# A third group of seven products in row block 3's first matmul, in place of four dense blocks

## The chip, the cores and the metric

The kernel runs on one core of a Trainium2 chip. The metric is device time in microseconds. Before the change it is 268.82 us, the median of three runs (268.22 to 269.44).

## What is computed

Two parts follow one another. Attention runs inside chunks of 64 tokens, for 8 batches, 8 heads, 576 tokens and head size 64. Its output is laid out as 4608 rows of 512 and goes through a two-layer network with an exact gelu:

```
q_c, k_c, v_c = (a.reshape(B, H, nc, 64, D) for a in (q, k, v))
scores = scale * np.matmul(q_c, k_c.transpose(0, 1, 2, 4, 3))
attn = softmax(scores)
out = np.matmul(attn, v_c)

x = out.transpose(0, 2, 1, 3).reshape(4608, 512)
h = x @ w_in                       # 512 -> 2048
g = 0.5 * h * (1 + erf(h / sqrt(2)))
return g @ w_out                   # 2048 -> 512
```

## The kernel before

**Row blocks.** The 4608 rows are worked in nine row blocks of 512, indices 0 to 8 (`t` in the code). Blocks 0 to 7 are the first 512 tokens of each batch, block 8 is the last chunk of all batches. For each block there are three stages: attention, which gives `x` transposed; mm1, which gives the gelu of h in a tile `h` of 16 feature blocks of 128 by 512 tokens; and mm2, which gives the output rows. Attention of block t+1 (and the scores of t+2) is laid in pieces between the steps of mm2 of block t.

**mm1 of one dense feature block** (`mm1_slot`, line 455): four matmuls of 512 columns, one for each quarter of the 512 inputs, into one PSUM bank. A gelu on ScalarE (ACT) takes the bank to `h` (line 457).

**mm1 by seven products** (`seven_rows`, line 573): four feature blocks at a time form a group. The group is a matrix of two by two blocks, and its product with the two-by-two blocks of x is made from seven block products in place of eight, the way of Strassen and Winograd. Each product is four matmuls of 256 columns on TensorE (PE). The sums that it needs are made ahead on VectorE (DVE): sums of w_in once for each group (`w_in_sums`), sums of x once for each row block (`x_sums`, line 556). The rest are steps of the group, named in the order lists:

- p1, p2, p3, p4, p6, p7: a product, added into a PSUM bank called a, b or d. p3 ends with the gelu of block (1, 0).
- p5: a product into d, and a copy on ACT of d into a tile in SBUF, `kept_p5` (line 585).
- s11: a copy on ACT of bank a to bank b (line 586). c11, c12, c22: gelus on ACT (line 581).
- s12: d becomes a + kept, on DVE (line 577). c22+: kept becomes a + kept, on DVE.

One prime on a name stands for the second group (feature blocks 4 to 7), two for the third (8 to 11), three for the fourth (12 to 15). A number in a list is a dense feature block.

**What sets the order.** Everything stands in a manual schedule: each engine works its instructions strictly in the order in which the program names them, and `mm1_seven` runs down one list for each row block. Other names in the lists are hooks: x is the x sums, k the copies of k by chunk for block 4 together with block 5's k transpose and the next loads, g0 sums of g for mm2 and two rounds of w_in sums.

**Banks and homes.** PSUM has eight banks in three pools: `mm` and `at` with three, `tp` with two. A new tile takes the place that was freed first, and waits until it is free. The kept tiles of groups one and two are in the pool `work`. From row block 5 on there are two more homes, `kept_more`, in a tile that is put aside in row block 4 (`kept_home`). The pool `ypool` has four tiles of 128 x 512 f32; mm2 uses four of them for each row block, for three kept products and the last one. Each of them is freed by the store of its quarter to HBM (`store_block`, line 743), which goes through the queue of SyncE (SP), in the order of the program, like nearly all loads.

**mm2** (`mm2_seven`, line 731) is one such group of seven over the whole block: first a product kept by a copy on ACT (line 691), then one into bank b, then five with sums. The third needs the first bank free, that is, the copy done. Row blocks 2 to 8 have mm1 with two or more groups. In row block 3 (`T0`), before the change, groups one and two are products and blocks 8 to 15 are dense.

Of the kernel before, what the change touches and what calls it, by code (L numbers as in the profile page):

```python
# [11 lines left out]
def kernel(  # L12
# [10 lines left out]
    P = 128  # L23
    f32 = mybir.dt.float32
# [14 lines left out]
    NT = B + 1  # L39
# [52 lines left out]
    ypool = ctx.enter_context(tc.tile_pool(name="ypool", bufs=4))  # L92
# [123 lines left out]
    AT, TP, MM = (ps_at, "at"), (ps_tp, "tp"), (ps_mm, "mm")  # L216
# [233 lines left out]
    def mm1_slot(t, f):  # L450
# [3 lines left out]
        for ks in range(KS):  # L454
# [5 lines left out]
    T0 = 3  # L460
    DENSE = (0,)
    TWICE = tuple(range(2, NT))
    THRICE = tuple(range(T0 + 2, NT))
    FOURTH = ("p1", "s11", 11, "p1'", "p2", "s11'", "c11", "p6", 9, "p5'", "p5", "p6'", 14, "s12'", "s12", "p2'", 13, 10, "p4'",
# [4 lines left out]
    LATER = ("p1", "s11", "p5", "p1'", "p1''", "p2", "p6", "c11", "s11'", "s11''", 13, "s12", 14, "p2''", "c11''", "p6'", "p4",  # L469
# [18 lines left out]
    LAST = ("p1", "p5", "s11", 13, 14, "p1'", "s11'", "p2", "c11", "p6", "p1''", "s11''", 15, "p5'", "s12", "p7", "p2''", "c22+",  # L488
# [3 lines left out]
    FOUR = {NT - 3: SIXTH, NT - 2: SEVENTH}  # L492
    WHOLE = {**FOUR, T0 + 1: FOURTH, NT - 1: LAST, T0 + 2: LATER}

    HF = FF // 2
    HD = d_model // 2
    HM = MT // P // 2
# [20 lines left out]
    def w_in_block(r, c, of=0):  # L518
        n = HD * (2 * of + r)
        return w_in_sb[:, 2 * c:2 * c + 2, n:n + HD]  # L520

    def x_block(t, r, c):
        return tiles[t]["x"][:, 2 * r:2 * r + 2, HD * c:HD * (c + 1)]

    def x_sum(i):
        return flat(k_bds[3 - (i - 1) // 2], 4)[:, (i - 1) % 2 * 2:(i - 1) % 2 * 2 + 2]
# [4 lines left out]
    kept_more = []  # L531
# [26 lines left out]
    def seven_rows(t, of, pools, kept, bank):  # L558

        h = tiles[t]["h"]  # L560
        w, ws = lambda r, c: w_in_block(r, c, of), w_in_sum[of]

        def place_of(to):
            if to not in bank:
                pool, tag = pools[to]
                bank[to] = pool.tile([P, HM, HD], f32, tag=tag, name="hs_ps")
            return bank[to]

        def product(to, left, right, fresh=False):
            hs = place_of(to)  # L570
            for f in range(HM):
                for ks in range(2):
                    nc.tensor.matmul(hs[:, f], left[:, ks, f * P:(f + 1) * P], right[:, ks],  # L573
                                     start=(fresh and f == 0 and ks == 0), stop=(ks == 1), skip_group_check=True)

        def plus(to, src):
            nc.vector.tensor_tensor(to, bank[src][:], kept, op=ADD)  # L577

        def gelu(r, c, src):
            n = HM * (2 * of + r)  # L580
            nc.scalar.activation(h[:, n:n + HM, HD * c:HD * (c + 1)], src, Act.Gelu)  # L581

        return {
            "p1": lambda: product("a", w(0, 0), x_block(t, 0, 0), True),
            "p5": lambda: (product("d", ws[0], x_sum(1), True), AC(kept, bank["d"][:])),
            "s11": lambda: AC(place_of("b")[:], bank["a"][:]),
            "p2": lambda: product("b", w(0, 1), x_block(t, 1, 0)),
            "c11": lambda: gelu(0, 0, bank["b"][:]),
            "p6": lambda: product("a", ws[1], x_sum(2)),
            "s12": lambda: plus(bank["d"][:], "a"),  # L590
            "p4": lambda: product("d", ws[3], x_block(t, 1, 1)),
            "c12": lambda: gelu(0, 1, bank["d"][:]),
            "p7": lambda: product("a", ws[2], x_sum(3)),
            "c22+": lambda: plus(kept, "a"),
            "c22": lambda: gelu(1, 1, kept),
            "p3": lambda: (product("a", w(1, 1), x_sum(4)), gelu(1, 0, bank["a"][:]))}

    def mm1_seven(t, hooks):

        if t > 1:  # L600
            tiles[t]["h"] = hpool.tile([P, FF, MT], bf16, tag="h", name="h")
        kept = [work.tile([P, HM, HD], f32, tag="t1", name="kept_p5", bufs=2)[:] for _ in range(2 if t in TWICE else 1)]
        bank, more, third, fourth = {}, {}, {}, {}
        if t == 1:
            does = seven_rows(t, 1, {"a": TP, "b": AT, "d": AT}, kept[0], bank)
        else:
            does = seven_rows(t, 0, {"a": AT, "b": AT, "d": AT}, kept[0], bank)
        if t in TWICE:
            does.update((step + "'", do) for step, do in
                        seven_rows(t, 1, {"a": TP, "b": TP, "d": AT}, kept[1], more).items())  # L610
            if t not in WHOLE:
                fifth = does["p5'"]
                does["p5'"] = lambda: (more.update(d=bank["b"]), fifth())
        if t in THRICE:
            pools = dict.fromkeys("abd", MM) if t == NT - 1 else {"a": MM, "b": AT, "d": AT}
            does.update((step + "''", do) for step, do in seven_rows(t, 2, pools, kept_more[0], third).items())
        if t in FOUR:
            does.update((step + "''", do) for step, do in seven_rows(t, 2, dict.fromkeys("abd", MM), kept_more[0], third).items())
            does.update((step + "'''", do) for step, do in
                        seven_rows(t, 3, {"a": MM, "b": AT, "d": MM} if t == NT - 2 else {"a": MM, "b": MM, "d": AT},  # L620
                                   kept_more[1], fourth).items())
        if t in WHOLE:
            order = WHOLE[t][:WHOLE[t].index("Y0")]
        elif t == T0:
            order = ("p1'", "s11'", "x", "p1", "s11", 8, 10, "k", "p6'", "p2", "c11", 11, "p6", "p5", "p5'", "p2'", "c11'", 9, 13,
                     "s12", "p7", "s12'", "p4", "c22+", "p7'", "c12", "c22", "p4'", "c12'", 15, "p3", "c22+'", "p3'", "c22'", 12,
                     "g0", 14)
        elif t == 2:
            order = ("p1", "s11", "p1'", "x", "u0", "s11'", 8, "p2", "c11", "p5", 9, "p6", "s12", "p5'", "p6'", "s12'", 10, "p7", 11,
                     "c22+", "c22", "p7'", 12, "p4", "c12", "p3", "c22+'", "p3'", 13, "p4'", "p2'", "u1", "k", "c22'", "c11'", "c12'",  # L630
                     "g0", 14, 15, "s3")
        else:
            order = (9, "p1", "s11", 10, 11, "w", "p5", "p2", "c11", "p6", 12, "s12", "w0", "p4", "p7", "c12", "c22+", "w1", 13,
                     "c22", "p3", 14, "g0", "s3", 15)
        for step in order:
            if step in does:
                does[step]()
                continue
            for u in hooks.get(step, ()):
                u()  # L640
            if not isinstance(step, str):
                mm1_slot(t, step)
# [224 lines left out]
    with tc.manual_schedule():  # L867
# [46 lines left out]
        p2 = att_sum_pe(0, 2)  # L914
        p3 = att_sum_pe(0, 3)
# [63 lines left out]
        def whole_hooks(t):  # L979
# [16 lines left out]
            e1, e2, slot = {}, {}, 0  # L996
            for step in WHOLE[t]:
                if str(step)[0] == "Y":
# [26 lines left out]
        for t in range(1, NT):  # L1025
# [46 lines left out]
            if t <= T0:  # L1072
# [24 lines left out]
                else:  # L1097
# [3 lines left out]
                    e2[13] = parts[1]  # L1101
            if t in WHOLE:
                e1, e2 = whole_hooks(t)
# [29 lines left out]
```

## Time and profile before

| | us |
|---|---|
| median of 3 runs | 268.82 |
| the profiled execution | 269.02 |
| its span, first to last instruction | 267.2 |
| PE busy | 258.7 (97%) |
| DVE busy | 220.8 (83%) |
| ACT busy | 199.1 (75%) |
| POOL busy | 87.8 (33%) |
| mm1 of row block 3 on PE | 106.18 to 119.29 |

The granted clock of PE is 1.00 throughout. Busy time is that in which an engine's datapath works; a wait is not counted in it. In a timeline, a group's length runs from its first start to its last end, and neighbours overlap, so the distance between two starts is what one more instruction costs. In the chain of work that ended last, each piece was released by the one ahead of it. SPq is the queue in which SP issues transfers; its landing is the time at which the transfer's semaphore tells that it is done.

### The profile page before, as it was taken

Reading aid. Unit: us, or ns where it says so; the run is one execution under the profiler, and the core shown is the slowest. Engines: PE = TensorE matmul, PEld = TensorE weight load, DVE = VectorE, ACT = ScalarE, POOL = GpSimd, SP = SyncE. Lnnn points to the kernel's source line nnn. Section 1 sums busy time; section 2 is a strip of 40 time slices with the busy share of each in tenths; the row PEclk is TensorE's granted clock in tenths of the full one; section 3 lists DMA queues with packets and bytes.
Section 4 is the critical chain, followed back from the end, with each engine's and each line's share of the span. In section 5 each row is a group of like instructions: output and inputs, shape, how many; then the busy total and the mean of one; then the engine's idle time right before and its main releaser. Section 6 shows DMA issues by size and latency. Waiting matters only on the chain.

```text
span 267.2 us, 7499 instructions
## 1 busy us (share of the span) xinstructions
PE 258.7 (97%) x3025; PEld 201.2 (75%) x3025; DVE 220.8 (83%) x373; ACT 199.1 (75%) x388; POOL 87.8 (33%) x142
## 2 busy tenths in 40 slices
PE   6699999999999999999999999999999999999994
PEld 2478775556886688668876887788888888887883
DVE  6874687989996899988998899898999999943752
ACT  3767758888676967789977987897799789228810
POOL 7878668701177210921712910304200300000000
PEclk9999999999999999999999999999999999999999
DMA  6999998999699899999899729999954320120014
GB/s 188 293 336 403 391 403 201 292 179 277 195 383 254 183 226 296 245 250 333 221 257 328 184 84 175 204 151 174 254 125 93 96 81 2 42 91 28 4 39 118
DMA packets 104739, 53.97 MB, mean 202 GB/s; under 512 B 72960, under 2 KB 101632, under 8 KB 104704
## 3 DMA queue, kind: packets, MB, share of 16 engines
q1 hardware_dynamic: 104400, 53.23, 76.6%
q8 instruction: 23, 0.38, 0.6%
q10 hardware_dynamic: 304, 0.26, 0.3%
q14 instruction: 12, 0.10, 0.1%
HBM read 36.70 MB, written 9.44 MB: 173 GB/s over the span
## 4 chain that ended last, share of the span: by engine, by line
PE 66%; DMA 14%; SPq 7%; DVE 6%; ACT 3%; issue 1%; POOL 1%; DVEq 0%; POOLq 0%
PE y_ps L731 27%; PE hs_ps L573 22%; PE h_ps L455 9%; DMA arrival<-in_moe_w_out_dram 5%; DMA arrival<-in_k_dram 5%; DMA arrival<-in_moe_w_in_dram 3%; SPq L157 2%; SPq L118 2%; SPq L128 2%; PE h_ps L445 2%; DMA k_t<-k_nat 1%; PE y_ps L801 1%; PE y_ps L765 1%; DVE k_bd L667 1%; PE av_ps L312 1%
## 5 line engine op out<-in xcount | busy, mean ns | idle before, releaser
L731 PEld LDWEIGHTS <-h 128*128 128x128 bf16 x384 | 37.1, 98 | 5.1 <-issue 0.4
L457 ACT ACTIVATE h<-h_ps 128x512 bf16<-128x512 f32 x53 | 31.7, 601 | 11.8 <-PE h_ps L455 7.7
L581 ACT ACTIVATE h<-hs_ps 128x512 bf16<-128x512 f32 x63 | 36.0, 602 | 3.7 <-PE hs_ps L573 3.4
L455 PE MATMUL h_ps<-x,w_in_sb 128*128 128x512 bf16 x156 | 38.6, 379 | 0.0
L164 POOL CAST q_nat<-arrival 128x512 bf16<-128x512 f32 x31 | 20.0, 686 | 52.3 <-DMA arrival<-in_q_dram 38.6
L214 POOL CAST v_nat<-arrival 128x1024 bf16<-128x1024 f32 x14 | 15.9, 1146 | 45.3 <-DMA arrival<-in_v_dram 45.3
L731 PE MATMUL y_ps<-v_bd,k_bd 128*128 128x256 bf16 x256 | 29.8, 273 | 0.2
L731 PE MATMUL y_ps<-w_out_sb,h 128*128 128x256 bf16 x256 | 29.8, 273 | 0.0
L573 PEld LDWEIGHTS <-w_in_sb 128*128 128x128 bf16 x252 | 24.6, 98 | 4.6 <-issue 0.2
L731 PEld LDWEIGHTS <-k_bd 128*128 128x128 bf16 x256 | 24.8, 98 | 3.7 <-issue 0.2
L164 POOL CAST k_nat<-arrival 128x512 bf16<-128x512 f32 x30 | 20.2, 706 | 17.3 <-DMA arrival<-in_v_dram 13.2
L455 PEld LDWEIGHTS <-w_in_sb 128*128 128x128 bf16 x156 | 15.3, 98 | 12.2
L573 PE MATMUL hs_ps<-x,w_in_sb 128*128 128x256 bf16 x168 | 23.6, 273 | 0.0
L696 DVE TENSOR_TENSOR kept<-y_ps,kept 128x512 f32<-128x512 f32 (+1 forms) x25 | 16.4, 656 | 6.7 <-issue 4.2
L865 ACT ACT_TABLE_LOAD x16 | 20.5, 1283 | 1.0 <-PEq L1117 0.7
L691 ACT COPY kept<-y_ps 128x512 f32<-128x512 f32 (+1 forms) x26 | 14.4, 558 | 9.2 <-PE y_ps L731 8.9
L577 DVE TENSOR_TENSOR hs_ps<-hs_ps,kept_p 128x512 f32<-128x512 f32 x15 | 10.2, 693 | 7.6 <-PE hs_ps L573 6.7
L731 PE MATMUL y_ps<-v_bd,s_sb 128*128 128x256 bf16 x128 | 15.8, 273 | 0.0
L246 ACT ACTIVATE pT<-s_ps 128x512 bf16<-128x512 f32 x28 | 14.4, 599 | 1.6 <-PE s_ps L239 1.6
L731 PE MATMUL y_ps<-v_bd,h 128*128 128x256 bf16 x128 | 15.3, 272 | 0.1
L573 PEld LDWEIGHTS <-w_in_more 128*128 128x128 bf16 x128 | 12.5, 98 | 3.7 <-issue 0.3
L731 PE MATMUL y_ps<-w_out_sb,s 128*128 128x256 bf16 x128 | 15.3, 273 | 0.0
(144 smaller groups left out, 553.0 us busy)
## 6 DMA issues: line engine op xcount, KB each, us to landing
arrival<-in_v_dram SPq DMA_DIRECT2D x58, 128.0 KB, 4.2
arrival<-in_q_dram SPq DMA_DIRECT2D x7, 1024.0 KB, 6.1
arrival<-in_k_dram SPq DMA_DIRECT2D x6, 1024.0 KB, 8.1
out_dram<-kept SPq DMA_DIRECT2D x21, 256.0 KB, 2.5
arrival<-in_moe_w_out_dram SPq DMA_DIRECT2D x4, 1024.0 KB, 12.1
arrival<-in_moe_w_in_dram SPq DMA_DIRECT2D x6, 512.0 KB, 6.5
out_dram<-y_sb SPq DMA_DIRECT2D x11, 256.0 KB, 3.0
arrival<-in_k_dram SPq DMA_DIRECT2D x8, 256.0 KB, 5.6
```

The lines of the kernel that those rows point to most:

```text
L164: copy(st[nm][:, g].rearrange("p j r d -> p r j d"), st[nm + "f"][:, 2 * g:2 * g + 2])
L214: copy(st["v"][:, r::2], st["vf"][:, r::2])
L246: nc.scalar.activation(pT[:].rearrange("p u (c j) -> p u c j", j=J), s_ps[g2][c][:].rearrange("p u (j c) -> p u c j", j=J), Act.Exp, scale ...
L455: (nc.tensor.matmul if t else by_halves)(h_ps[:], w_in_sb[:, ks, f * P:(f + 1) * P], tiles[t]["x"][:, ks, :], start=(ks == 0), stop=(ks == ...
L457: nc.scalar.activation(tiles[t]["h"][:, f, :], h_ps[:], Act.Gelu)
L573: nc.tensor.matmul(hs[:, f], left[:, ks, f * P:(f + 1) * P], right[:, ks], start=(fresh and f == 0 and ks == 0), stop=(ks == 1), skip_grou ...
L577: nc.vector.tensor_tensor(to, bank[src][:], kept, op=ADD)
L581: nc.scalar.activation(h[:, n:n + HM, HD * c:HD * (c + 1)], src, Act.Gelu)
L691: nc.scalar.copy(kept[name][:, ms], ps[:])
L696: nc.vector.tensor_tensor(y_sb[:, ms], ps[:], y_sb[:, ms], op=ADD)
L731: nc.tensor.matmul(to, left(f, m), right[:, f], start=(fresh and (split or m == 0) and f == 0), stop=(f == HF - 1), skip_group_check=True)
L865: nc.scalar.activation(act_scratch[:], rest[:, 0:1], func)
```

## The change

In row block 3 the feature blocks 8 to 11 become a third group of seven products; only 12 to 15 stay dense. The banks are a: `mm`, b: `at`, d: `at`. There is no `kept_more` yet in row block 3, so the group's kept product takes a tile of `ypool`. The order list of row block 3's mm1 is another one. The second group of row block 3 now takes a d bank of its own from `at`; before, it shared the first group's b bank. The pools of further groups of blocks 5 to 8 move into one table, `FURTHER`, with the same values.

```diff
-    THRICE = tuple(range(T0 + 2, NT))
...
-    FOUR = {NT - 3: SIXTH, NT - 2: SEVENTH}
-    WHOLE = {**FOUR, T0 + 1: FOURTH, NT - 1: LAST, T0 + 2: LATER}
+    WHOLE = {T0 + 1: FOURTH, T0 + 2: LATER, NT - 3: SIXTH, NT - 2: SEVENTH, NT - 1: LAST}
+    FURTHER = {T0: ((MM, AT, AT),),
+               T0 + 2: ((MM, AT, AT),), NT - 3: ((MM, MM, MM), (MM, MM, AT)),
+               NT - 2: ((MM, MM, MM), (MM, AT, MM)), NT - 1: ((MM, MM, MM),)}
...
-            if t not in WHOLE:
+            if t == 2:
                 fifth = does["p5'"]
                 does["p5'"] = lambda: (more.update(d=bank["b"]), fifth())
-        if t in THRICE:
-            pools = dict.fromkeys("abd", MM) if t == NT - 1 else {"a": MM, "b": AT, "d": AT}
-            does.update((step + "''", do) for step, do in seven_rows(t, 2, pools, kept_more[0], third).items())
-        if t in FOUR:
...
+        for of, pools in enumerate(FURTHER.get(t, ()), 2):
+            if kept_more:
+                home = kept_more[of - 2]
+            else:
+                home = ypool.tile([P, HM, HD], f32, tag="y", name="kept_p5")[:]
+            does.update((step + "'" * of, do) for step, do in seven_rows(t, of, dict(zip("abd", pools)), home, {}).items())
...
         elif t == T0:
-            order = ("p1'", "s11'", "x", "p1", "s11", 8, 10, "k", "p6'", "p2", "c11", 11, "p6", "p5", "p5'", "p2'", "c11'", 9, 13,
-                     "s12", "p7", "s12'", "p4", "c22+", "p7'", "c12", "c22", "p4'", "c12'", 15, "p3", "c22+'", "p3'", "c22'", 12,
-                     "g0", 14)
+            order = ("x", "p1", "s11", "p1'", "p1''", "s11'", "p5", "p6", "p2", "p6'", "s12", "k", "c11", "s11''", 14, "p4",
+                     "c12", "p2''", "p6''", "c11''", "p7", "p5''", "s12''", "p2'", "c22+", "c11'", "p5'", 12, "c22", 15, "s12'",
+                     "p7''", "p4''", "p7'", "p4'", "c22+''", "c12''", "c22''", "c22+'", "p3''", "p3", "p3'", "g0", "c12'", "c22'",
+                     13)
```

More of the change, by code (lines that the diff above doesn't have):

```diff
@@ L602, in mm1_seven @@
         kept = [work.tile([P, HM, HD], f32, tag="t1", name="kept_p5", bufs=2)[:] for _ in range(2 if t in TWICE else 1)]
-        bank, more, third, fourth = {}, {}, {}, {}
+        bank, more = {}, {}
         if t == 1:
@@ L610, in mm1_seven @@
                         seven_rows(t, 1, {"a": TP, "b": TP, "d": AT}, kept[1], more).items())
-            if t not in WHOLE:
+            if t == 2:
                 fifth = does["p5'"]
                 does["p5'"] = lambda: (more.update(d=bank["b"]), fifth())
-        if t in THRICE:
-            pools = dict.fromkeys("abd", MM) if t == NT - 1 else {"a": MM, "b": AT, "d": AT}
-            does.update((step + "''", do) for step, do in seven_rows(t, 2, pools, kept_more[0], third).items())
-        if t in FOUR:
[L618 to L621, printed above, removed]
+        for of, pools in enumerate(FURTHER.get(t, ()), 2):
[4 more added lines that the diff above has]
+            does.update((step + "'" * of, do) for step, do in seven_rows(t, of, dict(zip("abd", pools)), home, {}).items())
         if t in WHOLE:
```

## The prediction

> **What bounds the kernel now.** I read the busy table first, then the chain of work that ended last in order of time, then the timelines of the engines around row block 3, and last the DMA queue's timeline.
>
> ```profile
> PE 258.7 (97%) x3025; PEld 201.2 (75%) x3025; DVE 220.8 (83%) x373; ACT 199.1 (75%) x388; POOL 87.8 (33%) x142
> ```
>
> TensorE (PE) is busy 97% of the span, so whoever makes it stand sets the end. The chain says where it stood near the change; columns are start, length, what:
>
> ```profile
> 117.63 1.74 PE h_ps L455 x8
> ...
> 119.40 0.60 ACT h L457
> ...
> 120.01 1.28 ACT L865
> ...
> 121.41 0.92 ACT pT L246 x2
> ...
> 122.37 1.08 ACT pT L246 x2
> 123.45 0.49 ACT kept L691
> ...
> 123.98 1.03 PE y_ps L731 x8
> ```
>
> The mm1 of row block 3 runs on PE from 106.18 (its first hs_ps matmul) to 119.29. Then the chain leaves PE: the last gelu of h on ACT, the exp table, four exponentials, the copy of the first kept product, and only at 123.98 PE's third step of mm2. From 123.98 to 263.6 the chain holds PE alone, and the list of PE's waits has none in that stretch. So two things follow: what the change does to the end is what it does to the start of that step at 123.98, and that start hangs on ACT's last gelu, at 119.40. PE itself is there hardly earlier: its previous work ends at 123.93.
>
> The sizes come from the timelines of PE, ACT and DVE in that stretch (start, length of the group, count at the end):
>
> ```profile
> 111.82 0.60 PE L573 MATMUL hs_ps<-x,w_in_sb 128*128 128x256 bf16 x4
> 112.26 1.89 PE L455 MATMUL h_ps<-x,w_in_sb 128*128 128x512 bf16 x8
> 113.99 0.60 PE L573 MATMUL hs_ps<-k_bd,w_out_sb 128*128 128x256 bf16 x4
> ```
>
> ```profile
> 117.29 1.08 ACT L581 ACTIVATE h<-hs_ps 128x512 bf16<-128x512 f32 x2
> 118.24 0.64 ACT L581 ACTIVATE h<-kept_p 128x512 bf16<-128x512 f32 x1
> ```
>
> ```profile
> 108.82 3.83 DVE L207 COPY k_c<-k_t 128x512 bf16<-128x512 bf16 x4
> 112.56 1.28 DVE L577 TENSOR_TENSOR hs_ps<-hs_ps,kept_p 128x512 f32<-128x512 f32 x2
> ```
>
> Starts matter more than lengths, since neighbours overlap. Four matmuls of 256 columns: 112.26 - 111.82 = 0.44 us, 0.109 each. Eight of 512 columns: 113.99 - 112.26 = 1.73, 0.2165 each. A result can be read 0.16 after its last matmul's slot (0.60 - 0.44). ACT takes one tile after another every 0.48 (118.24 - 117.29 for two), each 0.6 long. DVE's additions follow each other at 0.61 (1.28 for two of 0.69).
>
> The last view is the queue that sends data out, with the issue row of the one store at 112.25:
>
> ```profile
> 101.61 10.54 SPq L128 DMA_DIRECT2D arrival<-in_v_dram  x9
> 112.25 0.55 SPq L743 DMA_DIRECT2D out_dram<-kept  x1
> ```
>
> ```profile
> out_dram<-kept SPq DMA_DIRECT2D x1, 256.0 KB, 2.5
> ```
>
> The first store of row block 2 was summed on DVE at about 99, but stands in SP's queue behind nine v loads; it is issued at 112.25 and lands 2.5 later, at 114.7.
>
> **The change, part by part.**
>
> *PE.* Dense blocks 8 to 11 go: 4 x 4 matmuls of 512 columns, 16 x 0.2165 = 3.46 us. Seven products of four matmuls of 256 columns come: 28 x 0.109 = 3.05. PE's own work falls by 0.41 us. (A page speaks against this part: the Trainium skill, "TensorE: Matmul & The Clock Gate", section "Back-to-back issue gap", gives streams of weight load and matmul 131 ns a matmul at 512 columns and 81 at 128; an estimate for 256, a third of the way between them, is some 98. By it the exchange would cost 28 x 0.098 - 16 x 0.131 = 0.65 in place of saving 0.41, and the sum below would be about +2.2. The rows disagree with it: 216 and 109.)
>
> *ACT.* The gelus stay in number: four of dense blocks against four of quarters. Two copies are new, s11'' and the keeping of p5'': 2 x 0.48 = 0.96 us. *DVE*: two additions are new, s12'' and c22+'', 2 x 0.61 = 1.2; DVE has the time, but its order matters below. The w_in sums of the third group exist already since row block 2, so they cost nothing here; POOL and SP keep their order.
>
> *The new wait.* The third group's kept product has no home of its own yet (kept_more is filled one row block later), so it takes a tile of the y pool, which has four. The next of the four to come free is the one of block (0, 0) of row block 2, and it is free when its store has landed. In the built order ACT's copy of p5'' is its ninth instruction of this mm1, and besides PE it waits for a DMA semaphore: that of exactly this store, the one issued at 112.25. So I walked the built orders of PE, ACT and DVE with the durations above, from PE at 106.18, ACT free at 106.96 (after the copy of y_sb), DVE at 108.74 (after the x sums).
>
> - PE without a stop: p1, p1', p1'', p5, p6, p2, p6' to 109.24, dense 14 to 110.10, p4, p2'', p6'', p7, p5'' to 112.28. s12 has its inputs at 108.7 and is done by 109.4, so p4 doesn't wait. Then p2', p5', dense 12 and 15 to 114.89.
> - ACT: eight instructions, the last c11'' at 111.28 to 111.88. p5'' can be read at 112.45; the store lands at 114.70. ACT stands for 2.25 us. Strict order puts 13 more of its instructions behind this one.
> - From 114.73 ACT has everything at hand or nearly: p5'' copy, c11', p5' copy, 12 at steps of 0.48; c22 at 116.68, since DVE does s12'' first (115.35) and c22+ next (to 116.65); 15, c12'', c22''; p3'' at 118.8, p3, p3', c12', c22', and the gelu of dense 13 at 121.3, in place of 119.40.
> - PE stands too: p7'' needs s12'' and starts at 116.07 in place of 114.89 (1.2 lost), p7' waits for s12' until 117.29 (0.3 lost). Its mm1 ends at 120.34 in place of 119.29, which is 1.5 lost less 0.4 saved. ACT is later than that, so this part is covered.
> - Behind it all is as before: table, four exponentials, kept copy, PE at 123.98 + 1.9 = 125.9. PE's scores in between wait for banks until 120.9, and its two steps of mm2 are done by 124.8; they fit.
>
> So the sum is +1.9 us, one number: 2.25 of standing, 0.96 for the copies, less 1.3 of the 1.8 that ACT stands idle in this mm1 in the trace of before and no longer does. DVE's sums for mm2 (k_bd) end at 123.7 and S3 at 125.4, before they are read at 125.9 and later. Behind 125.9 PE has no gap to give the time back. (If ACT took 0.52 a tile, as the Trainium skill, "ScalarE: Activation LUTs", section "What ACT_TABLE_LOAD costs", has it for 512 columns with an overlap of 93 ns, the 13 steps would add 0.5 and the sum would be +2.4; the timeline's 0.48 decides.)
>
> The price I can't see is the landing of that store in the changed run. All stores of this line land 2.2 to 5.7 us after issue, median 2.5 (its row by line): 114.45 to 117.95. That gives +1.6 to +5.1. I take 2.5, because it is this same store at this same place, and nothing ahead of it in SP's queue is changed.
>
> The profiled execution took 269.02, with 267.2 of span and 1.8 around it. 269.02 + 1.9 = 270.9; against the median of 268.82 it is 270.7. I say 270.8.
>
> **Rivals.**
>
> 1. *The wait costs nothing* (the other side: not slower). Place: ACT's copy of p5''. If the store had landed by 113.0, the copy could run at 112.48. Then ACT, with two more copies and five gelus queued behind PE's end, does its last gelu at 119.75: +0.2, 269.1. If ACT kept even with PE, only PE's saving would be left: -0.4, 268.6. The point from which it decides is a landing at 113.0; later than that, each us costs one. Against it: the store is issued only at 112.25, and none in the trace landed in under 2.2. For it: SP's queue could run earlier in another execution; 1.7 us would be needed.
> 2. *The store lands late*, since q, k and v loads share the engines: up to 117.95, +5.1, 274.1. Against it: from 96 to 136 us the six stores of kept products land after 2.7 (median) and the two of y_sb after 3.6.
> 3. *ACT gives time back*: gaps further on in mm2 of row block 3 absorb some. For it: ACT waits 0.2 at 130.6 for scores. Against it: that is after PE's start at 123.98, and PE's later steps follow without a gap. It would give +1.2 at the least, 270.2, and lies in the forecast's own range.
>
> **How the numbers follow.** Forecast with its third rival, +1.2 to +2.6 (270.0 to 271.6): 0.74. Rival 1, 268.6 to 269.3: 0.14. Rival 2, above 271.6: 0.12. The range reaches into both: 269.0 to 272.2. A measurement of this kernel tells 0.5% (1.3 us) from no change. Slower by more: 0.74 x 0.9 and rival 2 give 0.78; within: the rest of the forecast and most of rival 1, 0.19; faster: 0.03.
>
> **What would show it.** Right: an idle stretch of ACT of about 2.2 us before the copy of p5'' that ends when the store of line 743 lands; PE's p7'' after a gap of about 1 us; ACT's last gelu about 1.9 later than 119.4, and PE's third step near 125.9. Wrong: that copy at 112.5, or a store landed before 113; or a last gelu late with PE's third step still near 124.

## The result and the profile after

The changed kernel takes 271.43 us, the median of seven runs (269.78 to 272.65); the kernel before takes 268.82 in the same comparison (268.22 to 269.58). The ratio is 1.0082, with an interval of 1.0055 to 1.011: slower by 2.6 us, where 2.0 had been forecast for the median. All times and ratios here are of fast runs; one run of experiment 3, more than 1.5% above the fastest of its kernel, counts as slow and is left out.

The profiled execution of the changed kernel took 271.43 as well, with 269.6 of span. The busy table of its page has TensorE (PE) at the same 258.8 us, in a span that is 2.4 longer:

```profile
PE 258.8 (96%) x3021; PEld 203.8 (76%) x3037; DVE 222.7 (83%) x375; ACT 200.0 (74%) x390; POOL 89.4 (33%) x142
```

So the page shows PE standing 2.4 us longer, and the question is where. The forecast named one place, the copy of p5'' on ScalarE (ACT). Here are the timelines of PE and of ACT in this execution (start, length, what, count, and in brackets the idle time before and who ended it). Row block 3 begins at 107.31; the first line is p5'', the last line of PE's is p7''. In the changed kernel the lines of `seven_rows` are one higher than before: 574, 578, 582 and 586.

```profile
112.98 0.60 PE L574 MATMUL hs_ps<-k_bd,arrival 128*128 128x256 bf16 x4
...
114.29 1.89 PE L455 MATMUL h_ps<-x,w_in_sb 128*128 128x512 bf16 x8
116.01 0.60 PE L574 MATMUL hs_ps<-k_bd,arrival 128*128 128x256 bf16 x4
```

```profile
113.61 0.59 ACT L586 COPY kept_p<-hs_ps 128x512 f32<-128x512 f32 x1 [0.61 <-PE hs_ps L574]
...
118.40 2.06 ACT L582 ACTIVATE h<-hs_ps 128x512 bf16<-128x512 f32 x4 [0.20 <-PE hs_ps L574]
120.32 0.65 ACT L582 ACTIVATE h<-kept_p 128x512 bf16<-128x512 f32 x1
120.84 0.62 ACT L457 ACTIVATE h<-h_ps 128x512 bf16<-128x512 f32 x1
```

The copy of p5'' starts at 113.61, 0.2 after the slot of its product's last matmul (112.98 + 4 x 0.109 = 113.42), and PE's p7'' follows the dense blocks at 116.01 without a gap. **In this execution there was no wait.** The reason is in the queue of SyncE (SP):

```profile
99.31 10.92 SPq L128 DMA_DIRECT2D arrival<-in_v_dram  x9
110.33 1.60 SPq L743 DMA_DIRECT2D out_dram<-kept  x3
```

The store is issued at 110.33 and lands 2.5 later, at 112.83. By the forecast's own sign, a store landed before 113, this execution speaks against it. Counted from the begin of row block 3 the landing is 5.52; in the profile that the forecast was made from it was 8.52. Measured from that begin, the last gelu comes at +13.53 (before: +13.22), PE's third step of mm2 at +18.14 (before: +17.81), and mm1 of row block 4 at +28.41 (before: +28.05).

The other 2 us lie elsewhere. 1.13 is the begin itself, 107.31 for 106.18: a part of the program that the change doesn't touch. And 0.95 is in mm2 of row block 5, which takes 14.70 for 13.75. PE's timeline there, before and after the change:

```profile
182.35 0.71 PE L239 MATMUL s_ps<-q_t,k_c 64*64 64x64 bf16 x64
```

```profile
183.83 0.67 PE L239 MATMUL s_ps<-q_t,k_c 64*64 64x64 bf16 x59
185.25 0.25 PE L239 MATMUL s_ps<-q_t,k_c 64*64 64x64 bf16 x5 [0.75 <-issue]
```

The 64 score matmuls pass in 0.71 us before the change; after it PE stops for 0.75 us behind the 59th, and no other engine is named as what it waits for. 1.13 + 0.36 + 0.95 is the 2.4 of the span. So a forecast that came out near the median had not been borne out by this trace, and the experiments had to say whether the wait exists at all.

### The profile page after: what moved, and what is told of

Read it like the earlier page. It is cut to its first block, busy times and chain, and to the rows that moved or that the text cites. A ratio compares the mean times of both kernels' runs of the same rounds, so it can differ in the third digit from the quotient of the medians.

```text
span 269.6 us, 7516 instructions
## 1 busy us (share of the span) xinstructions
PE 258.8 (96%) x3021; PEld 203.8 (76%) x3037; DVE 222.7 (83%) x375; ACT 200.0 (74%) x390; POOL 89.4 (33%) x142
## 4 chain that ended last, share of the span: by engine, by line
PE 80%; DVE 10%; ACT 4%; DMA 2%; issue 2%; SPq 1%; POOL 0%; DVEq 0%; POOLq 0%
PE y_ps L731 30%; PE hs_ps L574 23%; PE h_ps L455 9%; PE h_ps L429 5%; PE y_ps L801 3%; DVE k_bd L667 2%; DMA arrival<-in_k_dram 2%; ACT k_bd L188 2%; PE h_ps L445 2%; PE av_ps L312 1%; PE y_ps L765 1%; DVE s_sb L654 1%; PE rc_ps L390 1%; DVE rc L373 1%; PE y_ps L429 1%
## 5 line engine op out<-in xcount | busy, mean ns | idle before, releaser
L582 ACT ACTIVATE h<-hs_ps 128x512 bf16<-128x512 f32 x66 | 37.5, 603 | 3.7 <-PE hs_ps L574 3.1
L164 POOL CAST q_nat<-arrival 128x512 bf16<-128x512 f32 x31 | 21.0, 718 | 54.0 <-DMA arrival<-in_q_dram 37.8
L457 ACT ACTIVATE h<-h_ps 128x512 bf16<-128x512 f32 x49 | 29.3, 602 | 10.8 <-PE h_ps L455 6.8
L455 PE MATMUL h_ps<-x,w_in_sb 128*128 128x512 bf16 x129 | 33.4, 379 | 0.6
L214 POOL CAST v_nat<-arrival 128x1024 bf16<-128x1024 f32 x14 | 17.0, 1220 | 45.3 <-DMA arrival<-in_v_dram 44.7
L574 PE MATMUL hs_ps<-x,w_in_sb 128*128 128x256 bf16 x176 | 24.6, 273 | 0.0
L578 DVE TENSOR_TENSOR hs_ps<-hs_ps,kept_p 128x512 f32<-128x512 f32 x16 | 11.0, 693 | 8.2 <-PE hs_ps L574 7.0
```

The lines of the kernel that those rows point to most:

```text
L164: copy(st[nm][:, g].rearrange("p j r d -> p r j d"), st[nm + "f"][:, 2 * g:2 * g + 2])
L214: copy(st["v"][:, r::2], st["vf"][:, r::2])
L455: (nc.tensor.matmul if t else by_halves)(h_ps[:], w_in_sb[:, ks, f * P:(f + 1) * P], tiles[t]["x"][:, ks, :], start=(ks == 0), stop=(ks == ...
L457: nc.scalar.activation(tiles[t]["h"][:, f, :], h_ps[:], Act.Gelu)
```

## The experiments

Each run below is compared with the kernel before on the same chip. "Begin" is the start of row block 3 on PE; the table at the end of this section has all executions.

**1. Both kernels again.** No edit. 

> The kernel before, unchanged, to see how its executions spread. First theory (the wait on the store): 268.8, every execution within 0.5 of that, since there is no such wait in it. Rival (the start of the kernel decides): executions with a granted clock under 1.00 in the first 20 us take about 1.3 more, 270 and above, as the profiled execution of the changed kernel, whose row block 3 began 1.1 late.

> The changed kernel, unchanged. First theory: where row block 3 begins at 106.2, ACT's copy of p5'' waits for the store until about 114.7 and PE's third step of mm2 is at 125.7 to 125.9. Where it begins 1 late or more, no wait, and third step at 18.1 after the begin. Both come to 270.5 to 271.5 in all. Rival (ACT's two more copies alone): third step 18.1 after the begin in any case, so 269.1 where the clock is 1.00.

Measured: before 269.04, ratio 1.0002 (0.998 to 1.0024); changed 271.49, ratio 1.0098 (1.006 to 1.0135). The expectation for the kernel before, every execution within 0.5 of 268.8, failed: its twelve runs go from 268.40 to 270.29. The slowest has the lowest mean clock (0.992), as the rival has it, but those at a clock of 1.00 go from 268.40 to 269.85. This time the profiled execution of the changed kernel has the wait. SP's queue, ACT and PE, with the begin at 106.43:

```profile
102.14 10.54 SPq L128 DMA_DIRECT2D arrival<-in_v_dram  x9
112.78 1.60 SPq L743 DMA_DIRECT2D out_dram<-kept  x3
```

```profile
115.33 0.59 ACT L586 COPY kept_p<-hs_ps 128x512 f32<-128x512 f32 x1 [3.20 <-PE h_ps L455]
...
121.84 0.62 ACT L457 ACTIVATE h<-h_ps 128x512 bf16<-128x512 f32 x1
```

```profile
113.41 1.89 PE L455 MATMUL h_ps<-x,w_in_sb 128*128 128x512 bf16 x8
116.70 0.60 PE L574 MATMUL hs_ps<-k_bd,arrival 128*128 128x256 bf16 x4 [1.40 <-DVE hs_ps L578]
117.13 0.60 PE L574 MATMUL hs_ps<-x,arrival 128*128 128x256 bf16 x4
117.89 0.60 PE L574 MATMUL hs_ps<-k_bd,w_in_more 128*128 128x256 bf16 x4 [0.16 <-DVE hs_ps L578]
```

The store, issued at 112.78, lands at 115.25, and 0.08 later the copy starts, after 3.20 us of idle time. The bracket names PE's dense blocks, which ended about then; but in the execution above the copy ran before those blocks ended, so it doesn't need them. The expectation tied the wait to an early begin. That is not what decides: this execution begins at 106.43, and those without a wait (here and in experiment 5) begin at 107.31, 105.53 and 105.52. The chain of work that ended last runs over this copy, as forecast:

```profile
115.33 0.59 ACT kept_p L586
...
119.89 2.08 ACT h L582 x4
121.98 0.49 ACT h L457
122.47 0.02 issue
122.48 1.28 ACT L865
...
123.91 2.02 ACT pT L246 x4
125.93 0.49 ACT kept L691
126.41 0.04 issue
126.45 1.91 PE y_ps L731 x16
```

**2. A home of its own.** The third group's kept product goes to a tile that is free by then, so it waits for no store.

```diff
-                home = ypool.tile([P, HM, HD], f32, tag="y", name="kept_p5")[:]
+                home = work.tile([P, HM, HD], f32, tag="rc", name="kept_p5", bufs=4)[:]
```

> The changed kernel with the third group's kept product in a tile of the pool work, tag rc, which is free by then; no store is waited for. First theory: 1.5 less than the changed kernel where row block 3 begins at 106.2, so 269.1 in all; less than that in the median, 0.5 to 1.5. Rival (no wait in most executions): within 0.3 of the changed kernel.

Measured: 270.35, ratio 1.0055 (1.0027 to 1.0083), beside 271.49 for the changed kernel on the same chip. Last gelu at +13.53 and third step at +18.14. So the median is 1.1 us lower without the wait, within the 0.5 to 1.5 expected; but the intervals of the two ratios overlap, and experiment 4 asks the same in another way.

**3. The store later.** Row block 2's four stores move behind a transpose in SP's queue.

```diff
-    def store_block(t, r, c, y_sb):
+    put_off = []
+
+    def store_block(t, r, c, y_sb, now=False):
+        if t == T0 - 1 and not now:
+            put_off.append((t, r, c, y_sb))
+            return
...
                 flip(n + 1, "q")
+                for one in put_off:
+                    store_block(*one, now=True)
```

> The changed kernel with row block 2's four stores behind the q transpose of block 5 in SP's queue, where they are issued about 3 later. First theory: ACT's copy of p5'' ends its wait 3 later, at 117.7 where row block 3 begins at 106.2, third step at 128.7, 273.5 to 274 in all. Rival (the wait is slack, ACT's backlog is made elsewhere): within 0.5 of the changed kernel.

Measured: 272.74, the median of five runs, ratio 1.0135 (1.009 to 1.018), 1.3 above the changed kernel and less than expected; the two intervals overlap, so the medians alone don't prove the rise. In the profiled execution SP's queue ran early, so the landing is only at 114.67, 8.11 after the begin (106.56); the expected 3 us don't show in it. But here the trace names the store itself as what ACT waits for, 2.49 us:

```profile
114.75 0.59 ACT L586 COPY kept_p<-hs_ps 128x512 f32<-128x512 f32 x1 [2.49 <-DMA out_dram<-kept]
```

The third step comes at +19.31. Not all that this execution loses is the wait: from the third step to mm1 of block 4 it takes 11.19, for 10.27 to 10.46 in the executions of the changed kernel. There two of DVE's sums for mm2 took 0.98 and 1.63 us in place of 0.69 and 1.22, and PE stood 0.47 at a copy on ACT; why they took longer is open.

**4. The store earlier.** Block 4's nine v loads and their casts move behind row block 2's first store; the kept product stays in `ypool`.

```diff
+        if t == T0 - 1:
+            hooks[HM * 2] += [lambda: load_v_rows(t + 2), lambda: cast_v_rows(t + 2, PO)]
...
-                if n + 1 < NT:
+                if n + 1 < NT and t != T0 - 1:
```

> The changed kernel with block 4's nine v loads (and their casts) issued behind the first store of row block 2 in place of ahead of it, so that this store, and the tile it frees, no longer hangs on the pace of SP's queue. Theory (the wait on that landing makes the difference between the changed kernel's median and that of the version with a home of its own): the store lands by about 105 in every execution, the copy of p5'' never waits, PE's third step of mm2 begins 18.1 after row block 3's begin, and the time is that of the version with its own home: 270.0 to 270.4, ratio 1.003 to 1.006. Rival (the home in the work pool helped in another way, by where the tile lies): 271.2 to 271.6, as the changed kernel, with the third step at 18.1 all the same. Second rival: the nine v loads and their casts, now up to 10 us later, are late for mm2 of row block 3 (v of block 4 is read there): a gap of PE before the products of v, and 271 or more.

Measured: 270.2, ratio 1.0039 (1.0012 to 1.0065). The time is the one expected, that of the kernel with a home of its own, and so are no wait and +18.14. The landing is not:

```profile
102.29 1.15 SPq L745 DMA_DIRECT2D out_dram<-kept  x1
103.48 10.39 SPq L128 DMA_DIRECT2D arrival<-in_v_dram  x9
```

```profile
out_dram<-kept SPq DMA_DIRECT2D x1, 256.0 KB, 9.3
```

Issued 10 us earlier than in experiment 1, the store still lands only at 111.58, 9.3 after its issue (5.15 after the begin). It now stands directly behind two loads of q and k, issued at 100.99 and 101.62. The second rival does not show either: PE has no gap before the products of v. Two changes to the program, a home without a store and a store moved in the queue, give 1.0055 and 1.0039 in place of 1.0098 and 1.0082, and the home of its own gives 1.0033 in another measurement (experiment 8): all three lie below both, though most pairs of intervals overlap. What the two changes have in common is that neither waits in its profiled execution, so the wait is the likely cause of the difference. That the moved store is never waited for in the other runs was not seen.

**5. Two more executions of the changed kernel.** 

> The changed kernel itself, one more execution with a profile. Theory: the begin of PE's third step of mm2, counted from row block 3's begin, is +18.1 where row block 2's first store lands by +6.8, and later by about 0.9 us for each us that it lands later; the span is longer by as much. Rival: the third step does not go with the landing.

> As for the look before: the third step at +18.1 with a landing by +6.8, later with a later landing. Rival: no such relation.

Measured: 269.55 and 269.80 us, landings 5.47 and 5.46 after the begin, no wait, third step +18.14 in both. They ran on the chip of experiment 4 and are not above its 270.2: without the wait the changed kernel costs no more than the version with the moved store. Of four profiled executions of the changed kernel one has the wait. Over all executions with this home the third step goes with the landing: +18.14 at landings up to 5.52, +19.31 at 8.11, +20.03 at 8.82, that is 1.0 us for each us between the last two, which leads back to 6.9 as the landing from which it costs.

**6. ACT's copies.** Without a wait 0.3 us is left at the last gelu. Is it the two new copies? The third group does without its copy s11''.

```diff
-            "s11": lambda: AC(place_of("b")[:], bank["a"][:]),
-            "p2": lambda: product("b", w(0, 1), x_block(t, 1, 0)),
+            "s11": lambda: left_out or AC(place_of("b")[:], bank["a"][:]),
+            "p2": lambda: product("b", w(0, 1), x_block(t, 1, 0), left_out),
```

> The changed kernel with the kept product in its own home, and without the copy s11'' of the third group: p2'' starts its bank afresh, so block (0, 0) of the group lacks p1. ACT's tail theory: one ACT tile less, last gelu 0.4 to 0.5 earlier, 13.05 after the begin, third step 17.65. Rival (PE's end or DVE sets it): no change, 13.5 and 18.1.

Measured in one execution: last gelu +13.53 and third step +18.14, both unchanged. The idle 0.20 before ACT's four gelus at 118.40 in the changed kernel's profile says why: ACT had caught up with PE there, so a copy ahead of it lies in a gap. What follows PE is those gelus and the two behind them, six in 3.06 us (118.40 to 121.46).

**7. Another order.** The version of experiment 2, with an order in which fewer gelus are left when PE ends its mm1.

```diff
-            order = ("x", "p1", "s11", "p1'", "p1''", "s11'", "p5", "p6", "p2", "p6'", "s12", "k", "c11", "s11''", 14, "p4",
...
+            order = ("x", "p1", "s11", "p1'", "p1''", "s11'", "p5", "p6", "p2", "c11", "s12", 15, "s11''", 12, "p7", "p4", "p6''", "k",
+                     "p2''", "c22+", "c12", "c11''", "p5''", "s12''", "c22", "p6'", "p5'", "p3", "s12'", "p2'", "c11'", "p7''",
+                     "p4''", "p7'", "p4'", "c22+''", "c12''", "c22''", "c12'", "c22+'", "p3''", "c22'", 13, "p3'", 14, "g0")
```

> The changed kernel with the kept product in its own home and another order of row block 3's mm1: dense 15 and 12 early, 13 and 14 at the end, so that ACT has less behind PE's last matmul. Theory (without the wait the rest of row block 3's price is ACT's tail): ACT's last gelu 12.9 after the begin in place of 13.5, PE's third step of mm2 17.4 to 17.6 after it in place of 18.1, mm1 and mm2 of row block 3 together 27.6 to 27.9 against 28.6, and 28.05 to 28.26 in the kernel before. Rival (another limit in mm2 of row block 3, DVE's sums): the two together stay at 28.4 or more. In total, with the stop in block 5's scores left in, 269.3 to 269.8.

Measured: 270.21, ratio 1.0041 (1.0018 to 1.0063). The theory fell: last gelu +13.36, third step +17.94, and the two stages together 28.55 for 28.60. PE stood for 0.22 at 114.47 waiting for a sum on DVE, and what came earlier at the third step was not kept in mm2. That agrees with the rival's 28.4 or more; that DVE's sums are the limit in mm2 is not shown. The total is above the expected 269.3 to 269.8 as well.

**8. The stop in block 5: is it a matter of count?** The changed kernel has 2081 matmuls ahead of these scores, and in every execution so far that has the stop it is behind the 59th score, ahead of PE's 2141st matmul. The change adds 28 matmuls and takes 16 away, and each has its weight load: 24 instructions more, ahead of that place. So twelve matmuls of two columns, with nothing that reads them, were put at the kernel's start, into the kernel before and into the version of experiment 2.

```diff
+        few = ps_mm.tile([P, MT], f32, tag="mm", name="few")
+        for _ in range(12):
+            nc.tensor.matmul(few[:, 0:2], rest[:, 0:P], rest[:, 0:2], start=True, stop=True)
```

> The kernel before with twelve matmuls of two columns more, 24 instructions of PE, at the very start where PE waits for q. They write a bank that nothing reads. Theory of the stop in block 5's scores (PE's program is 24 instructions longer in the changed kernel, and one of its instructions then comes after the fetch of the next piece of program): the stop of 0.3 to 0.9 ahead of the 60th of 64 score matmuls shows here too, at about 183, and mm2 of row block 5 takes 14.2 to 14.9 in place of 13.75; the total 0.5 to 1 above the kernel before. Rival (the stop comes from the data or from the order of row block 3): no stop, 13.75.

> The changed kernel with the kept product in its own home, and the same twelve small matmuls at the start, so that PE's program is 48 instructions longer than the kernel before. Theory of the fetch: the stop moves off the scores of block 5 or changes its size; where it falls can't be told. Rival: the stop stays ahead of the 60th score matmul, mm2 of row block 5 at 14.2 to 14.9.

Measured: before with 24 more, 269.44, ratio 1.0029 (0.9999 to 1.0059); home of its own with 24 more, 269.95, ratio 1.0033 (1.001 to 1.0057). The timelines of PE, first the home of its own and then the same with 24 more:

```profile
182.24 0.67 PE L239 MATMUL s_ps<-q_t,k_c 64*64 64x64 bf16 x59
183.85 0.24 PE L239 MATMUL s_ps<-q_t,k_c 64*64 64x64 bf16 x5 [0.94 <-issue]
```

```profile
182.09 0.57 PE L239 MATMUL s_ps<-q_t,k_c 64*64 64x64 bf16 x47
183.72 0.34 PE L239 MATMUL s_ps<-q_t,k_c 64*64 64x64 bf16 x17 [1.06 <-issue]
```

Twelve matmuls more ahead, and the stop comes twelve matmuls earlier in the scores, behind the 47th: its place hangs on the count. In the kernel before with 24 more, a step shows behind the 59th score too, but of only 0.20 us; mm2 of block 5 takes 13.96 for 13.75, where 14.2 to 14.9 was expected. So the count says where the stop is, and something else how long it is.

**9. The stop moved out of the scores.** If the count decides, 70 matmuls more must carry that place out of the 64 scores. The warming matmuls at the start were cut into pieces, in the version of experiment 2.

```diff
+        step = 64 if n > 1 else MT
         for _ in range(n):
-            nc.tensor.matmul(warm[:], rest[:, 0:P], rest[:], start=True, stop=True)
+            for c in range(0, MT, step):
+                nc.tensor.matmul(warm[:, c:c + step], rest[:, 0:P], rest[:, c:c + step], start=True, stop=True)
```

> The version with a home of its own, with the ten warming matmuls of its first 7 us (512 columns each, no result used) cut into pieces of 64 columns: 70 more matmuls, 140 more instructions of PE with their weight loads, of as many columns in all. The 2141st matmul then falls 10 ahead of the 64 scores of mm2 of block 5, among matmuls of 256 columns. Theory (PE stops where the next piece of its program has not come, and only a burst of short matmuls outruns it): no stop among the scores, and mm2 of block 5 takes 13.8 to 14.0 us in place of 14.9, as before the change; the time falls to 269.3 to 269.7, ratio 1.001 to 1.003. Rival (the piece is fetched only when PE comes to the scores, wherever it begins): the stop stands ahead of the scores or behind them, with 0.9 to 1.1 us, mm2 of block 5 takes 14.7 to 15.0, and the time is that of the version with its own home, 270.0 to 270.4.

Measured: 269.88, ratio 1.0022 (1.0003 to 1.0041).

```profile
182.39 1.04 PE L731 MATMUL y_ps<-v_bd,s_sb 128*128 128x256 bf16 x8
183.36 0.71 PE L239 MATMUL s_ps<-q_t,k_c 64*64 64x64 bf16 x64
184.00 1.05 PE L731 MATMUL y_ps<-v_bd,s_sb 128*128 128x256 bf16 x8
```

All 64 scores in 0.71 and no stop; mm2 of block 5 is back at 13.75. The ratio lies in the expected range, the median 0.2 above it. The medians don't show what the stop costs, though: the same version with 24 more has the longest stop of all and 269.95. In the traces it is plain. In the profiled execution the begin is 1.22 later than that of experiment 2 (106.75 for 105.53) and the rest, from the begin to the end, 1.47 shorter (161.49 for 162.96). Whether the pieces at the start cause the later begin is open, since begins differ as much between executions of one kernel.

All profiled executions, in us; columns two to six count from the begin:

| | begin | landing | last gelu | third step | mm1 of block 4 | end | mm2 of block 5 |
|---|---|---|---|---|---|---|---|
| before | 106.18 | 8.52 | 13.22 | 17.81 | 28.05 | 161.04 | 13.75 |
| before, again | 106.17 | 6.64 | 13.42 | 18.01 | 28.26 | 161.23 | 13.74 |
| before, 24 more | 105.86 | 5.65 | 13.22 | 17.81 | 28.10 | 161.39 | 13.96 |
| changed | 107.31 | 5.52 | 13.53 | 18.14 | 28.41 | 162.33 | 14.70 |
| changed, again | 106.43 | 8.82 | 15.42 | 20.03 | 30.49 | 163.92 | 14.21 |
| changed, two more | 105.53, 105.52 | 5.47, 5.46 | 13.53 | 18.14 | 28.39, 28.60 | 162.23, 162.39 | 14.63, 14.59 |
| later store | 106.56 | 8.11 | 14.71 | 19.31 | 30.50 | 163.58 | 13.76 |
| earlier store | 106.43 | 5.15 | 13.53 | 18.14 | 28.38 | 162.68 | 14.61 |
| own home | 105.53 | 5.43 | 13.53 | 18.14 | 28.60 | 162.96 | 14.89 |
| own home, 24 more | 105.38 | 5.47 | 13.53 | 18.14 | 28.60 | 162.81 | 15.00 |
| own home, 140 more | 106.75 | 6.36 | 13.63 | 18.24 | 28.50 | 161.49 | 13.75 |
| own home, other order | 106.87 | 6.14 | 13.36 | 17.94 | 28.55 | 162.13 | 13.99 |
| without s11'' | 106.52 | 6.15 | 13.53 | 18.14 | 28.39 | 162.25 | 13.88 |

All other stages from block 4 on agree within 0.05, but for the last one of mm2 with the tail (16.04 to 16.8).

## Why the prediction was right, and where it was not

**The time** was right, 2.0 forecast and 2.6 measured between the medians, but it is a sum of other parts than the one that was forecast, so that it came out so near is in part luck.

**The walk of the wait** held, step by step, in the execution that has it. With the landing 0.30 later after the begin than assumed, it would give a last gelu at 121.3 - 106.18 + 0.30 = +15.42 (measured +15.42), p7'' at +10.19 (measured 116.70 - 106.43 = +10.27), p7' at +11.41 (measured +11.46), and PE's third step at +20.02 (measured +20.03).

**How likely the wait is** was mis-sized. The step that failed is the choice of the price: "I take 2.5, because it is this same store at this same place, and nothing ahead of it in SP's queue is changed". The 2.5 us of transfer held (2.4 to 2.7 wherever the v loads are ahead). But the issue is not fixed against the compute: SP's queue came through the same nine loads up to 3.4 us earlier in other executions (landings of 5.43 to 8.82 with this queue). The nine loads themselves take 10.5 to 11.5 us each time; the late executions come late to them (the k transpose ahead of them is issued at 97.03 and 97.81, for 93.77 to 96.19 in the others), and why is open. The landing of the unchanged kernel itself was 8.52, 6.64 and 5.65 after the begin in three executions. The one profile at hand was at the late end of that, and a forecast of 0.74 was hung on it; of four profiled executions of the changed kernel, one has the wait. Of the twelve executions with this order of the queue, two have such a landing: 8.52 and 8.82; the other ten are at 6.64 or earlier, as rival 1 needed. How many of the timed runs have the wait can't be read, since they leave no trace. The medians differ by 1.1 to 1.3 us (270.35 and 270.2 against 271.43 and 271.49). One wait in four at some 2 us (mm1 of block 4 at +30.49 for +28.39 to +28.60) would be 0.5 on average, so either more of the timed runs have it or something else adds to it; that stays open.

**Rival 1** therefore describes most profiled executions, and in row block 3 by its numbers (its total, 268.6 to 269.3, is under all three of them, 269.55 to 271.43): it gave the last gelu at 119.75, +13.57 after the begin, for +13.53 measured. Its point of decision, a landing 6.8 after the begin, agrees with the 6.9 that the later landings point back to; no execution with this home landed between 5.52 and 8.11, so the point itself was not seen. Its +0.2 measured +0.33 at the third step and +0.34 to +0.55 at mm1 of block 4; against the second execution of the kernel before (+18.01 and +28.26) it is only +0.13 and +0.13 to +0.34. One of the two copies behind the 0.96 in the forecast's sum was taken out and changed nothing when ACT doesn't wait (experiment 6). That leaves ACT's order at PE's end as the likely cause of this rest; experiment 7, which should have shown it, moved it by 0.2 in place of 0.6.

**PE's exchange** was right: mm1 without the wait ends, at the begin of the scores, at 120.03 - 107.31 = 12.72 after the begin, for 13.11 before; 0.39 saved, 0.41 forecast. Four matmuls of 256 columns still follow at 0.44 us. (The 98 ns that the Trainium skill, "TensorE: Matmul & The Clock Gate", section "Back-to-back issue gap", led to by the estimate do not show here either.) As forecast, this saving is covered by ACT.

**"Behind 125.9 PE has no gap"** failed, though in a place that the forecast didn't look at. The stop in the scores of block 5 made mm2 of that block longer by 0.84 to 1.26 us in six executions, by 0.46 in the one with the wait, by 0.13 to 0.25 in three others, and not at all with the later store. Its place comes from the change's number of instructions, not from its work. Without it the version with a home of its own is 1.14 us shorter in mm2 of block 5 by the traces; its median is 269.88 for 270.35, which is not clear of the noise. What is then left, 1.0022 or 0.6 us, is near the +0.45 of row block 3 (28.50 for 28.05).

So the 2.6 us are, as an estimate: 1.1 to 1.3 by the medians for the wait, 0.5 to 1 for the stop, up to 0.5 for ACT's tail, and what the starts differ by. That wait, stop and tail exist is shown by the traces; their shares of the median are not.

## What to carry to other kernels

A wait that hangs on a DMA's landing has no one price: read the landing against the compute in several executions, and give the wait a share of them before putting a number on it. A home that is freed by a store is only as early as the queue ahead of that store, so look for one that compute frees. And a change that alters an engine's instruction count can move a stop like that of block 5 into a burst of short instructions: look for such bursts further on.

## What the runs showed of the hardware

**PE stopped at a fixed count of its instructions.** The page of the version with a home of its own counts the packets of the queue that brings instructions:

```profile
q8 instruction: 24, 0.39, 0.6%
```

That is 16 KB a packet. PE and its weight loads have 6074 records there (3037 each): 0.39 MB over them is 64 bytes each, 256 to a packet, or 128 matmuls with their loads. In all ten executions with a step in the scores, PE goes on 1.30 to 1.61 us after the end of such a packet: with the home of its own the packet ends at 182.53, the scores begin at 182.24, and PE resumes at 183.85. How long PE stands goes with how early it comes: beginning the scores 0.29 before the packet's end it stopped most of a microsecond; 0.48 after it (the changed kernel with the wait) 0.27; 1.03 after it (the later store, 185.17 for 184.14) not at all: there the 60th score starts 1.51 after the packet's end, within the 1.30 to 1.61 after which PE goes on elsewhere. In the version of experiment 9 a packet came at 175.37, 8.0 ahead of the scores: some 70 matmuls of 0.11 us earlier, and no stop shows. The Trainium skill, "Runtime: NRT & Kernel Launch", section "Instruction fetch mechanics", has blocks of 16 KiB with 256 instructions, and the cost of crossing one "mostly hidden". The size agrees with this count; the stop was up to 1.06 us here. Shown is that its place goes with the count of instructions; that PE waits for this packet is read from the times alone, and what asks for the packet just then stays open.

**A store directly behind two loads of 1 MB took 9.3 us to land, for 2.5 behind nine small ones** (experiment 4, one execution). Issued 10 us earlier than in experiment 1, it landed 3.7 earlier (111.58 for 115.25); counted from the begin, it landed only 0.3 to 0.4 earlier than in the other three executions of the changed kernel (5.15 for 5.46 to 5.52).

**The start of the kernel differs by 1.9 us between executions** (begins of 105.38 to 107.31), and by 1.8 within the changed kernel (105.52 to 107.31). In the changed kernel's profile, a load of q came later, PE stood 1.47 us before it (0.78 before the change), and the granted clock fell to 0.67 for a stretch. Busy time of each engine and granted clock, before and after:

```profile
15.00:20.00 5.00, 4.96 (x70) 4.18 (x67) 3.68 (x8) 2.80 (x7) 3.64 (x8) 1.00 1.01 337
```

```profile
15.00:20.00 5.00, 5.00 (x68) 4.26 (x65) 3.15 (x7) 2.79 (x5) 3.37 (x8) 0.67 0.98 321
```

Medians of many runs average over this difference; a single pair of profiles doesn't, and 1.13 of the 2.4 us between the first two came from it.
